# Batch 0 of a cosine-attention and FNet block: fixed load order for K and Q, squares on three engines, W1 in seven transfers

## The chip, the core and the metric

The kernel runs on one core of one Trainium2 chip. The metric is the device time of one execution in microseconds, the median of several runs. The core has TensorE (PE in the profile, with its weight loads as PEld), VectorE (DVE), ScalarE (ACT), GpSimd (POOL) and SyncE (SP). PE multiplies into PSUM. Loads and stores are DMAs; here SP issues those of K and Q and the plain stores, POOL those of V and the weights (with a cast to bf16) and the indirect stores. Each engine runs its own instructions in order and waits on semaphores.

## What is computed

For 8 batches, 12 heads, 448 tokens and heads of 64: rows of q and k are normalised, scores are divided by tau = 0.1, then softmax and the product with v. The result, 448 x 768 a batch, goes through a mixing and an FFN:

```python
q_n = q / (np.linalg.norm(q, axis=-1, keepdims=True) + 1e-06)
k_n = k / (np.linalg.norm(k, axis=-1, keepdims=True) + 1e-06)
scores = np.matmul(q_n, k_n.transpose(0, 1, 3, 2)) / tau
attn = np.exp(scores - max);  attn = attn / (sum + 1e-09)
x = np.matmul(attn, v)                       # as (8, 448, 768)
u = x + real(fft(fft(x, axis=1), axis=2))
un = (u - mean) / sqrt(var + 1e-06)
out = u + np.maximum(un @ w_ch1, 0.0) @ w_ch2    # 768 -> 3072 -> 768
```

## The kernel before

The program is not written in the order in which it runs. Every step is an operation given to a planner (`Plan.add`): the engines that may do it, an estimated cost on each, a priority, what it reads and writes. `Plan.schedule` places the operations one after another at the earliest time that its estimates give, on one of the engines allowed, and among those ready then by priority. The order it finds per engine is emitted as it is, with the semaphore waits that the reads and writes need. So the order on the chip is fixed when the kernel is built, and an engine that waits for one operation holds all behind it. `TIMES` has measured costs, `FLOW` a model of loads (latency, service time, share), `SHIFT` (lines 82 on) a number for each operation that is added to its priority. `Plan.fill` puts matmuls of the identity (later of W1) into gaps of PE; they appear as line 2168.

Batch 0 runs like this. `consts` (line 974 on) makes, with iota on POOL, arguments of cosine and sine tables: for the 448 tokens (names ending in s) and for the 768 features (ending in d). DVE reduces the arguments (lines 1014 to 1023), ACT takes the sines (1050 to 1053), with a table load for sines before and one for logarithm and exponential behind (1058). The feature table's sines come late (1050, 1052), behind batch 0's exponentials, with table loads at 1060 and 1071; `sinp` (1064) makes its negated half.

`first_norm` (line 1109 on) loads K and Q in fp32 for pairs of heads in three groups: pair 0, pairs 1 and 2, pairs 3 to 5. Each group has three loads issued by SP at line 1157: K and Q for tokens 0 to 383 and a "tail" (two DMAs, q and k of the last 64 tokens). Squares are ACT's (1164), their sums over 64 DVE's (1167). `norms` then takes the root as logarithm and exponential on ACT (1103, 1105) and the reciprocal on DVE (1106, 1107). Scaling (1186, 1190) is on DVE or POOL. PE transposes (1213, 1225 to 1227, 1238), ACT or DVE copy the result out of PSUM into QK and KTD (1204, 1248).

`attn` loads V in four pieces by POOL (1333 to 1336), behind the load with index 4 in the order of the program, which is Q of pairs 1 and 2. For each pair of heads PE makes scores (1378, 1391), ACT four exponentials into one of two buffers E (1356), three of 900 columns and one of 450. PE multiplies with V (1409, 1415), DVE divides (1433, 1435). A pair's exponentials need the product with V of the pair before the last to be done, which frees the buffer.

`fold` (1452, 1459, 1486) uses the symmetry of the transform; `fsum` does the token part on PE (1534, 1543), copied out at 1564 and 1565; `fft` the feature part (1586), in two groups, then the sum u (1650), the layer norm (1680 to 1690) and its transposition (1700, 1708). `up` is the first FFN product (1775, evacuated at 1791), `prod` the second (1919).

`weights` (line 1074) loads W1 and W2 by POOL in 12 transfers each (1084, 1085). The first three wait for the third load of V, each later one for the landing of the third before it. K and Q of batch 1 wait for the first piece of W1 (`gate` in `first_norm`).

## Time and profile before

| | us |
|---|---|
| median of 3 runs | 579.37 |
| lowest and highest | 578.66, 581.11 |
| span of the profiled execution | 579.0 |
| DVE, ACT, POOL busy in it | 438.7, 383.0, 224.5 |

The profile is one execution on the chip, shown as a page (busy time, slices, the chain that ended last, the costliest groups) and as answers to questions about its trace: a timeline of instructions, the waits, busy time by stretch, DMA issues with their time to landing. In a timeline, the bracket behind an instruction is how long its engine sat idle before it, and who ended that. A line number is that of the kernel before.

### The profile page before, as it was taken

Reading aid. Unit: us, or ns where it says so; the run is one execution under the profiler, and the core shown is the slowest. Engines: PE = TensorE matmul, PEld = TensorE weight load, DVE = VectorE, ACT = ScalarE, POOL = GpSimd, SP = SyncE. Lnnn points to the kernel's source line nnn. Section 1 sums busy time; section 2 is a strip of 40 time slices with the busy share of each in tenths; the row PEclk is TensorE's granted clock in tenths of the full one; section 3 lists DMA queues with packets and bytes.
Section 4 is the critical chain, followed back from the end, with each engine's and each line's share of the span. In section 5 each row is a group of like instructions: output and inputs, shape, how many; then the busy total and the mean of one; then the engine's idle time right before and its main releaser. Section 6 shows DMA issues by size and latency. Waiting matters only on the chain. (4 is left out here: it accounts for less than half of the span.)

```text
span 579.0 us, 16019 instructions
## 1 busy us (share of the span) xinstructions
PE 557.0 (96%) x6610; PEld 435.4 (75%) x6610; DVE 438.7 (76%) x926; ACT 383.0 (66%) x722; POOL 224.5 (39%) x338
## 2 busy tenths in 40 slices
PE   3899899999999899999999999999999999999998
PEld 3668787677687587878778678687796886959695
DVE  8789977988459967895688769976789459987353
ACT  6789967465876795479747876586558652758171
POOL 8344422446426534623362536441642103031303
PEclk9799999999999999999999999999999999999999
DMA  9999995986339652964297239942590200122011
GB/s 193 204 228 156 168 181 105 185 173 121 91 96 104 138 125 61 167 137 110 64 129 133 63 109 139 125 128 52 138 91 16 84 1 1 57 42 71 14 43 55
DMA packets 187897, 62.19 MB, mean 107 GB/s; under 512 B 166800, under 2 KB 185616, under 8 KB 187824
## 3 DMA queue, kind: packets, MB, share of 16 engines
q0 software_dynamic: 57968, 22.81, 34.6%
q1 hardware_dynamic: 129856, 38.35, 33.2%
q8 instruction: 52, 0.85, 0.6%
q14 instruction: 21, 0.17, 0.1%
HBM read 51.90 MB, written 11.01 MB: 109 GB/s over the span
## 5 line engine op out<-in xcount | busy, mean ns | idle before, releaser
L1775 PE MATMUL PS<-UNT,W1b 128*128 128x256 bf16 (+1 forms) x1728 | 186.0, 264 | 1.6 <-DVE TX L1791 0.4
L1775 PEld LDWEIGHTS PS<-UNT,W1b 128*128 128x128 bf16 x1728 | 153.1, 98 | 22.4 <-issue 2.2
L1356 ACT ACTIVATE E<-PS 128x900 bf16<-128x900 f32 (+1 forms) x192 | 148.6, 826 | 29.7 <-PE PS L1378 24.4
L1919 PE MATMUL PS<-W2b,HQ 128*128 128x384 bf16 x720 | 125.0, 326 | 0.7 <-DVE HQ L2019 0.7
L1301 POOL TENSOR_TENSOR QH<-STG,SM 128x256 bf16<-128x256 f32 x126 | 81.6, 673 | 82.6 <-DVE SM L1107 58.1
L1919 PEld LDWEIGHTS PS<-W2b,HQ 128*128 128x128 bf16 x720 | 68.8, 98 | 44.4 <-DVE HQ L2019 1.1
L1945 POOL TENSOR_TENSOR OUTB<-OUTB,U 128x192 f32<-128x192 f32 x72 | 50.8, 725 | 127.6 <-ACT OUTB L1940 111.4
L1919 PE MATMUL PS<-TX,HQ 128*128 128x384 bf16 (+2 forms) x444 | 76.7, 322 | 1.3 <-DVE OUTB L1956 1.0
L1791 ACT ACTIVATE HQ<-PS 128x512 bf16<-128x512 f32 x85 | 50.6, 595 | 40.9 <-PE PS L1775 40.2
L2019 DVE TENSOR_TENSOR HQ<-HQ 128x1536 bf16<-128x1536 bf16 (+1 forms) x73 | 56.0, 771 | 11.2 <-ACT HQ L1791 6.8
L1919 PEld LDWEIGHTS PS<-TX,HQ 128*128 128x128 bf16 x444 | 41.4, 98 | 28.0 <-DVE OUTB L1956 2.2
L1290 DVE TENSOR_REDUCE SM<-QH 128x6 f32<-128x384 f32 x84 | 45.2, 547 | 13.1 <-ACT QH L1288 12.6
L1288 ACT ACTIVATE QH<-STG 128x384 f32<-128x384 f32 x84 | 42.6, 519 | 18.9 <-DVE SM L1290 17.3
L1415 PE MATMUL PS<-VB,E 128*128 128x65 bf16 x1152 | 52.4, 194 | 0.0
...
L1415 PEld LDWEIGHTS PS<-VB,E 128*128 128x128 bf16 x1152 | 48.6, 98 | 1.3
L1791 DVE TENSOR_SCALAR HQ<-PS 128x512 bf16<-128x512 f32 x41 | 28.2, 687 | 21.7 <-PE PS L1775 21.6
L1378 PE MATMUL PS<-QK 64*128 64x225 bf16 (+2 forms) x864 | 39.4, 229 | 3.1 <-ACT QK L1204 2.0
L1409 PE MATMUL PS<-VZ,E 128*128 128x130 bf16 x192 | 41.9, 221 | 0.2
L1638 DVE SCALAR_TENSOR_TENSOR U<-ACG,X 128x768 bf16<-128x768 f32 (+4 forms) x39 | 38.9, 1006 | 0.7
L1940 ACT ACTIVATE OUTB<-PS 128x384 f32<-128x384 f32 x36 | 17.6, 490 | 31.3 <-PE PS L1919 31.3
L1378 PEld LDWEIGHTS PS<-QK 64*128 64x128 bf16 x864 | 26.0, 95 | 15.7 <-issue 8.5
...
## 6 DMA issues: line engine op xcount, KB each, us to landing
STG<-in_q_dram SPq DMA_DIRECT2D x18, 384.0 KB, 4.0
STG<-in_k_dram SPq DMA_DIRECT2D x18, 384.0 KB, 4.4
VB<-in_v_dram POOLq DMA_DIRECT2D x24, 192.0 KB, 7.1
W1b<-in_moe_w_ch_dram POOLq DMA_DIRECT2D x12, 384.0 KB, 7.8
W2b<-in_moe_w_ch_dram POOLq DMA_DIRECT2D x12, 384.0 KB, 6.7
out_dram<-OUTB SPq DMA_DIRECT2D x7, 384.0 KB, 2.9
...
```

What stands on the lines that cost most here:

```text
L1288: P.add("act", lambda a, sq=sq, src=buf[:, w * x:w * x + w]: a.activation(sq, src, ACTF.Square), t_act(w), pr, f"sq{i}_{b}", reads=bn, wri ...
L1290: P.add("dve", lambda v, o=SS[:, i, H // ns * x:H // ns * (x + 1)], sq=sq: v.tensor_reduce(o, sq.rearrange("p (h d) -> p h d", d=DH), AX.X ...
L1301: r = v.tensor_tensor(v3(qh)[:, h:h + 4], v3(buf)[:, h:h + 4], RN[:, i, h:h + 4].unsqueeze(2).to_broadcast((128, 4, DH)), AluOp.mult)
L1356: return a.activation(o, self.PS[:, bk:bk + nc_, 0:SQ2], ACTF.Exp, scale=1.0 / self.tau)
L1378: i = pe.matmul(self.PS[:, bk + h, c0:c0 + n], self.KT[r, jj, kt * 128:(kt + 1) * 128], self.QT[r, jj, cols], start=True, stop=True)
L1409: r = pe.matmul(o, st(6), self.VZ[:, j, :], start=not split, stop=(split and i == 0), skip_group_check=True)
L1415: r = pe.matmul(o[:, 65 * h:65 * h + 65], st(2 * kt + h), self.VB[:, kt, 2 * j + h, :], start=(split and i == h == kt == 0), stop=((not sp ...
L1775: r = pe.matmul(self.PS[:, bk, x * n:(x + 1) * n], self.W1b[:, j, ft * 128:(ft + 1) * 128], self.UNT[:, j, cs], start=(j == 0), stop=(j == ...
L1791: return e.activation(o, i, ACTF.Relu) if e is self.nc.scalar else e.tensor_relu(o, i)
L1919: r = pe.matmul(self.PS[:, bk, 0:n], lhs(f), rhs(f), start=(start and f == 0), stop=(stop and f == NF // 2 - 1), skip_group_check=True)
L1945: r = g.tensor_tensor(self.OUTB[:, ob, xs], self.OUTB[:, ob, xs], self.U[:, ut, xs], AluOp.add)
L2019: P.add("dve", lambda v: v.tensor_tensor(cs(o), cs(a), cs(bq), op), 0.16 + 0.3 * len(ks), -0.5, f"{nm}{ks[0]}_{b}", reads=rd, writes=[x fo ...
```

## The change

K and Q of batch 0 are loaded in the order K, Q, tail (now for pairs 0 to 2), K and Q of pairs 1 and 2, K, Q and tail of pairs 3 to 5, each load ordered behind the one before it. V waits for the landing of K of pairs 1 and 2. Squares of batch 0 may be on ACT or DVE, those of the last group on POOL too, and the last group's squares of K and Q are made pair by pair. The first arguments of the feature table may be on POOL and have a later priority; the negated sine table is read by the second group of the feature transform, and the groups change places. The first subtraction and addition of the last fold are halved, and one half needs only an earlier pair. W1 comes in two narrow and five double transfers, W2 as before. A table `HOME` fixes the engine of some 70 operations, among them the negated table and scalings of batch 0. All numbers in `SHIFT` are new, for all batches. The two iotas of the first operation are parted.

```diff
--- before.py
+++ after.py
...
 SHIFT = {
...
+HOME = {
+    "tqd": {0: "dve", 1: "dve"}, "trd": {0: "dve"}, "tas": {0: "act"}, "sinp": {0: "dve"}, "half": {0: "pool", 1: "act"}, "sqK0_0": {0: "act"},
+    "sqQ0_0": {0: "act"}, "sqT0_0": {0: "dve"}, "scK0_0": {0: "dve"}, "scQ0_0": {0: "dve"}, "scT0_0": {0: "dve"}, "ek0_0": {0: "act"},
+    "eq0_0": {0: "act"}, "et0_0": {0: "dve", 1: "act"}, "sqK1_0": {0: "dve"}, "scK1_0": {0: "dve"}, "scQ1_0": {0: "dve"}, "scT1_0": {0: "dve"},
+    "scK2_0": {0: "dve"}, "scQ2_0": {0: "dve"}, "scT2_0": {0: "dve"}, "ek1_0": {0: "dve"}, "eq2_0": {0: "act"}, "et1_0": {0: "dve", 1: "act"},
+    "sqK2_0": {1: "act", 2: "dve"}, "sqQ2_0": {0: "act", 1: "act", 2: "act"}, "sqT2_0": {0: "act"}, "scK3_0": {0: "dve"}, "scQ3_0": {0: "pool"},
+    "scT3_0": {0: "dve"}, "scK4_0": {0: "pool"}, "scQ4_0": {0: "dve"}, "scK5_0": {0: "pool"}, "scQ5_0": {0: "pool"}, "scT5_0": {0: "pool"},
+    "ek3_0": {0: "dve"}, "eq3_0": {0: "act"}, "eq4_0": {0: "dve"}, "ek5_0": {0: "act"}, "eq5_0": {0: "dve"}, "et2_0": {0: "dve"}, "gc2_0": {0: "dve"},
...
+}
...
-            g.iota(kcf, [[1, NK]], base=0, channel_multiplier=0, allow_small_or_imprecise_dtypes=True)
             for t in range(2):
                 r = g.iota(self.rowf[:, t:t + 1], [[0, 1]], base=128 * t, channel_multiplier=1, allow_small_or_imprecise_dtypes=True)
             return r
+
+        def iotak(g):
+            return g.iota(kcf, [[1, NK]], base=0, channel_multiplier=0, allow_small_or_imprecise_dtypes=True)
...
-        P.add("pool", iotas, 0.5, -19, "iota", writes=["OUT1", "OUT1b", "rowf"])
+        P.add("pool", iotas, 0.25, -19, "iota", writes=["rowf"])
+        P.add("pool", iotak, 0.4, -19, "iotak", writes=["OUT1", "OUT1b"])
...
-            m = (c.stop - c.start) // 2
+            m, es = (c.stop - c.start) // 2, ("dve", "pool") if nm == "d" else ("dve",)
             xs = [slice(c.start + t * m, c.start + t * m + m) for t in range(2)]
             for t, x in enumerate(xs):
-                P.add("dve", lambda v, x=x, t=t: v.tensor_scalar(Qt[:, x], col, self.rowf[:, k + t:k + t + 1], M, AluOp.mult, AluOp.add),
-                      t_arg(m), pr, "tq" + nm, reads=rd + ["rown"], writes=[f"tq{nm}{t}"])
+                P.add(es, lambda v, x=x, t=t: v.tensor_scalar(Qt[:, x], col, self.rowf[:, k + t:k + t + 1], M, AluOp.mult, AluOp.add),
+                      (t_arg(m), 0.2 + 0.0024 * m)[:len(es)], pr, "tq" + nm, reads=rd + ["rown"], writes=[f"tq{nm}{t}"])
             qs = [f"tq{nm}{t}" for t in range(2)]
-            P.add("dve", lambda v: v.tensor_scalar(Qt[:, c], Qt[:, c], M, -float(n), AluOp.subtract, AluOp.mult),
-                  t_arg(2 * m), pr, "tr" + nm, reads=qs, writes=qs)
+            P.add(es, lambda v: v.tensor_scalar(Qt[:, c], Qt[:, c], M, -float(n), AluOp.subtract, AluOp.mult),
+                  (t_arg(2 * m), 0.2 + 0.0048 * m)[:len(es)], pr, "tr" + nm, reads=qs, writes=qs)
...
-        arg(sd, lcf, DM, 2, -5, "d", ["OUT1d", "rowf"])
+        arg(sd, lcf, DM, 2, 16, "d", ["OUT1d", "rowf"])
...
-            done = [table(sd, self.CSd, DM, 10, "d", [trig], "CSd")]
+            done = [table(sd, self.CSd, DM, 10, "d", [trig], "CSc")]
...
-        for i in range(24):
-            c = i % 12
-
-            def fn(g, s, i=i, c=c):
-                if i < 12:
-                    return g.dma_start(self.W1b[:, :, c * 256:(c + 1) * 256], w1[:, :, c * 256:(c + 1) * 256]).then_inc(s, 16)
-                return g.dma_start(self.W2b[:, c * 2:(c + 1) * 2, :], w2[:, c * 2:(c + 1) * 2, :]).then_inc(s, 16)
-            nm = f"W{1 + i // 12}_{c}"
-            prev.append(P.add("pool", fn, 0.8, 9, nm, writes=[nm], dma=(nm, 16), after=[prev[-3]], serve=2.1))
-        self.w = prev[3:]
+        self.w = []
+        for i, (x, c0, c1) in enumerate([(0, 0, 1), (0, 1, 2)] + [(0, c, c + 2) for c in range(2, 12, 2)] + [(1, c, c + 1) for c in range(12)]):
+            def fn(g, s, x=x, c0=c0, c1=c1):
+                if x == 0:
+                    return g.dma_start(self.W1b[:, :, c0 * 256:c1 * 256], w1[:, :, c0 * 256:c1 * 256]).then_inc(s, 16)
+                return g.dma_start(self.W2b[:, c0 * 2:c1 * 2, :], w2[:, c0 * 2:c1 * 2, :]).then_inc(s, 16)
+            nm = [f"W{1 + x}_{c}" for c in range(c0, c1)]
+            prev.append(P.add("pool", fn, 0.8, 9, nm[0] if c1 - c0 == 1 else f"W1w_{c0}", writes=nm, dma=(nm[0], 16), after=[prev[-3]], serve=2.1))
+            self.w += prev[-1:] * (c1 - c0)
...
+            nt = (3, 0, 3)[g] if b == 0 else n
+            R3 = hf[:, o + 2304 + 128 * ja:o + 2304 + 128 * (ja + nt)]
             L = [("k", [(heads(K, n), self.heads(self.k, b, 2 * a, 2 * n, 0, 3, 128, 192))], 0.64 * n),
-                 ("q", [(heads(Q, n), self.heads(self.q, b, 2 * a, 2 * n, 0, 3, 128, 192))], 0.64 * n),
-                 ("t", [(heads(R[0:64], n), self.heads(self.q, b, 2 * a, 2 * n, 384, 1, 64, DH)),
-                        (heads(R[64:128], n), self.heads(self.k, b, 2 * a, 2 * n, 384, 1, 64, DH))], 0.3 * n)]
-            parts.append((g, a, n, L, [("K", K, [f"Sk{g}_{b}"]), ("Q", Q, [f"Sq{g}_{b}"]), ("T", R, [f"St{g}_{b}"])]))
+                 ("q", [(heads(Q, n), self.heads(self.q, b, 2 * a, 2 * n, 0, 3, 128, 192))], 0.64 * n)]
+            if nt:
+                L += [("t", [(heads(R3[0:64], nt), self.heads(self.q, b, 2 * a, 2 * nt, 384, 1, 64, DH)),
+                             (heads(R3[64:128], nt), self.heads(self.k, b, 2 * a, 2 * nt, 384, 1, 64, DH))], 0.3 * nt)]
+            gt = 0 if b == 0 and g == 1 else g
+            parts.append((g, a, n, nt, R3, L, [("K", K, [f"Sk{g}_{b}"]), ("Q", Q, [f"Sq{g}_{b}"]), ("T", R, [f"St{gt}_{b}"])]))
         sc, ID = [], self.ID
-        for g, a, n, L, ps in parts:
+        for g, a, n, nt, R3, L, ps in parts:
             for nm, dm, sv in L:
                 def fn(sy, sem, dm=dm):
                     for dst, src in dm:
                         sy.dma_start(dst, src).then_inc(sem, 16)
-                self.loads.append(P.add("sp", fn, 0.36 * len(dm), pg[g], f"ld_{nm}{g}_{b}", writes=[f"S{nm}{g}_{b}"],
-                                        dma=(f"lh{g}{nm}{b}", 16 * len(dm)), serve=sv, after=gate))
+                self.loads.append(P.add("sp", fn, (0.36 if b else 0.55) * len(dm), pg[g], f"ld_{nm}{g}_{b}", writes=[f"S{nm}{g}_{b}"],
+                                        dma=(f"lh{g}{nm}{b}", 16 * len(dm)), serve=sv, after=gate, order=self.loads[-1:] if b == 0 else ()))
+                if (b, g, nm) == (0, 1, "k"):
+                    self.vgate = self.loads[-1]
             red, rn = [], [[f"RN_{a + j}{i}" for j in range(n)] for i in range(3)]
             for i, (nm, buf, names) in enumerate(ps):
-                w = wd[i] * n
-                sq = sqb[i][0][:, sqb[i][1] + wd[i] * a:sqb[i][1] + wd[i] * (a + n)] if b == 0 else sqs[g][i]
-                P.add("act", lambda e, sq=sq, buf=buf: e.activation(sq, buf, ACTF.Square), t_act(w), pg[g], f"sq{nm}{g}_{b}",
-                      reads=names, writes=sqn[g][i], order=[self.exps[-1]] if b else [])
-                out = SS.rearrange("p (j c) -> p j c", c=14)[:, a:a + n, 6 * i:6 * i + (6, 6, 2)[i]]
-                red.append(P.add("dve", lambda v, sq=sq, out=out, n=n: v.tensor_reduce(out, sq.rearrange("p (j h d) -> p j h d", j=n, d=DH), AX.X, AluOp.add),
-                                 t_dve(w), pg[g], f"ss{nm}{g}_{b}", reads=sqn[g][i], writes=[f"SS_{a + j}{i}" for j in range(n)], order=sc if b else []))
+                m, y = (n, buf) if i < 2 else (nt, R3)
+                if not m:
+                    continue
+                for j0, j1 in ((0, m),) if b or g < 2 else [(j, j + 1) for j in range(m)] if i < 2 else ((0, m),):
+                    w, u0, u1 = wd[i] * (j1 - j0), wd[i] * (a + j0), wd[i] * (a + j1)
+                    sq = sqb[i][0][:, sqb[i][1] + u0:sqb[i][1] + u1] if b == 0 else sqs[g][i]
+                    y_ = y[:, wd[i] * j0:wd[i] * j1]
+                    es = ("act",) if b else (("act", "dve"), ("act", "dve"), ("act", "dve", "pool"))[g]
+                    sn = sqn[g][i] if j0 == 0 else [f"{sqn[g][i][0]}_{j0}"]
+
+                    def square(e, sq=sq, y_=y_):
+                        return e.activation(sq, y_, ACTF.Square) if e is self.nc.scalar else e.tensor_tensor(sq, y_, y_, AluOp.mult)
+                    P.add(es, square, [{"act": t_act(w), "dve": t_dve(w), "pool": 0.1 + 0.0023 * w}[e] for e in es], pg[g], f"sq{nm}{g}_{b}",
+                          reads=names, writes=sn, order=[self.exps[-1]] if b else [])
+                    out = SS.rearrange("p (j c) -> p j c", c=14)[:, a + j0:a + j1, 6 * i:6 * i + (6, 6, 2)[i]]
+                    red.append(P.add("dve", lambda v, sq=sq, out=out, n=j1 - j0: v.tensor_reduce(out, sq.rearrange("p (j h d) -> p j h d", j=n, d=DH), AX.X, AluOp.add),
+                                     t_dve(w), pg[g], f"ss{nm}{g}_{b}", reads=sn, writes=[f"SS_{a + j}{i}" for j in range(j0, j1)], order=sc if b else []))
             self.norms(b, pg[g], 14 * a, 14 * (a + n), [f"SS_{a + j}{i}" for j in range(n) for i in range(3)], rn[0] + rn[1] + rn[2])
             if b == 0:
-                self.ssk.append(red[0])
+                self.ssk += red
...
-            gate = [self.loads[4]] if b == 0 else [self.w[11]] if b == 1 else []
+            gate = [self.vgate] if b == 0 else [self.w[11]] if b == 1 else []
...
-        for i, o in ((0, AluOp.add), (2, AluOp.subtract)):
-            P.add("dve", lambda v, i=i, o=o: v.tensor_tensor(AC[:, i:i + 2], X[:, 0:2], X[:, 2:4], o),
-                  t_dve(512, 2) + (0.05 if b else 0.0), pj, f"fa{dj}_{b}", reads=xr, writes=[f"AC{i}"], after=self.snu)
+        halves = [(slice(0, 2), xr, pj, [])] if b or dj != 1 else [(slice(0, 1), [f"X{dj}"], pj - 1, self.last_f), (slice(1, 2), xr[1:], pj, [])]
+        for h, rd, pf, af in halves:
+            for i, o in ((0, AluOp.add), (2, AluOp.subtract)):
+                P.add("dve", lambda v, i=i, o=o, h=h: v.tensor_tensor(AC[:, i:i + 2, h], X[:, 0:2, h], X[:, 2:4, h], o),
+                      t_dve(256 * (h.stop - h.start), 2) + (0.05 if b else 0.0), pf, f"fa{dj}_{b}", reads=rd, writes=[f"AC{i}" + "b" * (h.start == 1)] + [f"AC{i}b"] * (h.stop == 2), after=self.snu + af)
...
-            for sg in (0, 1) if b == 0 else (0,):
+            for sg in (1, 0) if b == 0 else (0,):
                 self.fd_ops.append(P.add("pe", fn if b else lambda pe, fn=fn, sg=sg: fn(pe, sums=(sg,)), 8 * (0.085 if b == 0 else 0.064), pr + 1, f"fd{kt}_{b}",
-                                         reads=["Tt0", "Tt1", "Tt1b", "CSd"] + (["CSp"] if b == 0 and sg else []),
-                                         tiles=(tile,), acquire=None if sg else tile, margin=0.2))
+                                         reads=["Tt0", "Tt1", "Tt1b"] + (["CSp", "CSc"] if b == 0 and sg else ["CSd"] + ["CSc"] * (b == 0)),
+                                         tiles=(tile,), acquire=None if b == 0 and not sg else tile, margin=0.2))
...
+            op.engs = (HOME[op.name][k],) if k in HOME.get(op.name, ()) else op.engs
```

Left out are the numbers of `SHIFT`, the rest of `HOME`, changes of names in the fold and reads of the feature table that follow from the above, and three costs.

More of the change, by code (lines that the diff above doesn't have):

```diff
@@ L82 @@
 SHIFT = {
-    "iota": {0: -676.9695}, "cst": {0: -75.5528}, "iotad": {0: -74.6806}, "rown": {0: 48.0599}, "tqd": {0: -682.9733, 1: -32.1767},
-    "trd": {0: 56.7288}, "tpd": {0: -32.1767, 1: -367.9451}, "tad": {0: 309.9105}, "tqs": {0: -30.877, 1: -174.0331}, "trs": {0: -286.881},
[4 rows of a table removed]
-    "ldt1": {0: 105.5066}, "sind": {0: -697.7679}, "mask": {0: 897.4065}, "sinp": {0: 23.8646}, "half": {0: -44.205, 1: 289.4036},
[457 rows of a table removed]
-}
-LATE = {r"W[12]_\d+": 1.5, "tmd": 2.0, r"sq\d_\d": 1.5, r"sq[KQT]\d_1": 1.5, r"ktd\d": 2.0, r"qdup\d": 2.0, r"qk\d._[2-7]": 1.5, r"pv\d\d_[2-7]": 1.5, r"pv\d\d_1": 1.0, r"h\d+_[1-7]": 0.5}
+    "iota": {0: -4743.9411}, "iotak": {0: -3749.0012}, "cst": {0: 2295.738}, "iotad": {0: 1504.4864}, "rown": {0: 3564.9514},
@@ L1070, in tables @@
                   e.tensor_scalar(self.CSn, self.CSs[:], -1.0, None, AluOp.mult), (t_act(4 * NK), 0.5, 2.5), 10, "sinn", reads=["CSs"], writes=["CSn"])
-            self.ldt = P.add("act", lambda a: a.preload_act_table_set("natural_log_exp_and_others"), 1.3, 10, "ldt", order=done)
+            self.ldt = P.add("act", lambda a: a.preload_act_table_set("natural_log_exp_and_others"), 1.3, 28, "ldt", order=done)
         self.tables = tables
@@ L1204, in ev @@
                     return e.activation(dst, i, ACTF.Copy) if e is self.nc.scalar else e.tensor_copy(dst, i)
-                self.evac(ev, n, pg[g] + 0.1 * (jj - a), nm, b == 0 and jj > 2, writes=wr, after=(tile.users[0],), tiles=(tile,))
+                self.evac(ev, n, pg[g] + 0.1 * (jj - a), nm, False, writes=wr, after=(tile.users[0],), tiles=(tile,))
             for j in range(n):
@@ L1464, in fold @@
                 self.first_f = op
+            self.last_f = [op]
         if dj < 2 and b == 0 and not direct:
```

18 lines of the change are left out of this document (13 added, 5 removed), and 975 rows, old and new, of the table SHIFT.

## Prediction

> **What bounds the kernel now.** I read the page first: the span and the engines' shares.
>
> ```profile
> span 579.0 us, 16019 instructions
> PE 557.0 (96%) x6610; PEld 435.4 (75%) x6610; DVE 438.7 (76%) x926; ACT 383.0 (66%) x722; POOL 224.5 (39%) x338
> ```
>
> PE is busy 96% of the span, so what can be won is PE time that does no product of the result. Some of the busy time is padding: line 2168 is a matmul of the identity that only keeps PE running. So I took the busy time of each engine in three stretches, and then that of line 2168 alone (columns: stretch, us, busy us of PE, PEld, DVE, ACT and POOL; in the last two rows PE alone).
>
> ```profile
> 0.00:50.00 50.00, 36.51 (x495) 29.19 (x496) 41.05 (x97) 38.91 (x58) 26.96 (x58) 0.93 1.26 197
> 50.00:100.00 50.00, 48.01 (x662) 39.91 (x661) 40.89 (x99) 38.69 (x75) 15.44 (x22) 1.00 1.09 157
> 100.00:579.00 479.00, 472.43 (x5457) 366.25 (x5454) 356.81 (x732) 305.36 (x589) 182.12 (x260) 1.00 0.58 93
> ...
> 0.00:50.00 50.00, 12.47 (x138) 0.93 1.26 197
> 50.00:100.00 50.00, 1.50 (x18) 1.00 1.09 157
> ```
>
> Lost to PE: in the first 50 us 50 - 36.51 + 12.47 = 26.0 us, in the next 50 us 2.0 + 1.5 = 3.5, in the other 479 us 6.6. Products are the same before and after the change, so the time falls by about what the first 50 us lose less, as long as the rest stays as full as it is. That is where the edits lie; the new priorities after 100 us can win at most 6.6 us and I count them at nothing.
>
> Next the timeline of the first 53 us, by engine, to see which wait holds the attention of batch 0; here are picked rows of SP's DMA issues and of ACT (start, duration, instruction, idle time before it and who ended it).
>
> ```profile
> 0.72 0.45 SPq L1157 DMA_DIRECT2D TX<-in_q_dram  x1
> 1.23 0.49 SPq L1157 DMA_DIRECT2D TX<-in_k_dram  x1
> 1.77 1.23 SPq L1157 DMA_DIRECT2D TX<-in_q_dram  x2
> 7.69 1.28 ACT L1058 ACT_TABLE_LOAD   x1
> 8.98 0.31 ACT L1103 ACTIVATE SM<-SM,MV 128x14 f32<-128x14 f32 x1
> 16.54 0.52 ACT L1164 ACTIVATE HQ<-TX 128x384 f32<-128x384 f32 x1 [1.96 <-DMA TX<-in_k_dram]
> 16.97 0.47 ACT L1204 ACTIVATE QK<-PS 128x384 bf16<-128x384 f32 x1
> 17.91 1.73 ACT L1356 ACTIVATE E<-PS 128x900 bf16<-128x900 f32 x2 [0.47 <-PE PS L1378]
> 25.48 0.92 ACT L1356 ACTIVATE E<-PS 128x900 bf16<-128x900 f32 x1 [1.28 <-PE PS L1378]
> 33.32 7.94 ACT L1356 ACTIVATE E<-PS 128x900 bf16<-128x900 f32 x11 [0.51 <-PE PS L1378]
> ```
>
> ACT is in order. The copy of K of pair 0 (16.97) stands behind a square (16.54) that waits 1.96 us for a load of pairs 3 to 5, which pair 0 doesn't need. So the first exponential starts at 17.91; the last ends at 33.32 + 7.94 = 41.26. The first product of the FFN comes 11.1 us later:
>
> ```profile
> 52.39 5.55 PE L1775 MATMUL PS<-UNT,W1b 128*128 128x128 bf16 x96
> ```
>
> **The change part by part.** *A, the way to the first exponential.* K0, Q0 and a tail load for three pairs now lead the queue, V waits, and the arguments of the feature table leave the head of DVE.
>
> ```profile
> 9.82 0.24 DVE L1107 RECIPROCAL SM<-SM 128x14 f32<-128x14 f32 x1
> 10.62 0.54 DVE L1190 TENSOR_TENSOR QH<-TX,SM 128x384 bf16<-128x384 f32 x1
> 18.39 0.29 DVE L1186 TENSOR_TENSOR TX<-TX,SM 128x128 bf16<-128x128 f32 x1
> ```
>
> ```profile
> TX<-in_k_dram SPq DMA_DIRECT2D x1, 192.0 KB, 3.4
> TX<-in_q_dram SPq DMA_DIRECT2D x1, 192.0 KB, 3.7
> TX<-in_q_dram SPq DMA_DIRECT2D x1, 96.0 KB, 6.8
> ```
>
> With the issue times of the first three slots, K0 lands at 0.72 + 3.4 = 4.1 and Q0 at 1.23 + 3.7 = 4.9. The two DMAs of the wider tail are issued from 1.77 to 3.0; their size, 96 KB, took 6.8 in a full queue, and twice the size took 3.4 in an empty one. I take 4, nearer to the empty queue that it now has: 6.4 from the second issue at about 2.4. A square and a sum of some 0.5 each: 7.4. The table load that ended at 8.97 must also be over; it stood behind sines that waited for DVE, whose queue loses the feature table, so I let it be hidden. From the logarithm at 8.98 to the end of the reciprocal (10.06) took 1.1: 8.5. Three scalings on DVE, 0.54 + 0.29 + 0.54 = 1.4, all of pair 0 on DVE now: 9.9. Then transposing and copying Q, about 1.0 by the copy's 0.47 and as much on PE, and scores, 0.5: the first exponential at 11.4, **6.5 us** earlier. Bounds: 4.5 (the tail takes 6.8) to 7.5.
>
> V's five DMAs (POOL) move behind the landing of K1. Behind them on POOL stand iotas of the store indices, the clearing of KTD and all of W1:
>
> ```profile
> 15.60 0.88 POOL L1084 DMA_DIRECT2D W1b<-in_moe_w_ch_dram  x1 [0.55 <-POOL IDX L1036]
> 48.11 2.55 POOL L1084 DMA_DIRECT2D W1b<-in_moe_w_ch_dram  x3 [0.55 <-POOL CS L1064]
> DMA to landing us min/median/max: 5.7/7.8/11.1
> ```
>
> ```profile
> VB<-in_v_dram POOLq DMA_DIRECT2D x3, 192.0 KB, 11.5
> TX<-in_k_dram SPq DMA_DIRECT2D x1, 384.0 KB, 7.0
> GB/s 0 0 0 26 100 333 370 353 331 188 101 63 261 338 344 347 369 301 223 171 160 143 148 126 117 76 119 226 263 254 222 161 161 167 164 151 169 175 185 127
> ```
>
> The first fence is POOL's W1 issues and their time to landing; in the second, the last column of the first two lines is us to landing, and the last line is the first 20 us in slices of 0.5. K and Q alone moved at 330 to 370 GB/s at 2.5 to 4.5 us, and at 120 to 225 after 9 us, when V ran beside them. With V held back all of K and Q (2 x 12 x 448 x 64 x 4 bytes = 2.75 MB) need some 8 us at that pace: about 10. K1, fifth in the queue and issued near 3.2, lands between 6 by the pace and 10.2 by its row's 7.0. V took 11.5 from issue to landing while it shared; with less to share it should land by 17. It is first needed when the third pair's exponentials want the first buffer again, after two pairs of exponentials, some 6 us after 11.4, so it is covered by less than 1 us. If it lands later it is the next thing that is late.
>
> *B, the exponentials.* 24 are needed; by the stretch of 11 in 7.94 that is 17.3 us. The phase lasted 23.35, so 6.0 were other work and waits. In the change pair 0 starts before the squares of the later pairs are done, so more work of ACT falls inside: five squares of 0.52 (Q2 in three, T2, one of K2), two pairs of logarithm and exponential (0.5 each), four copies of 0.47: 5.5. The rest of the squares goes to DVE. Waits I put at 2.5, since no square waits for a late load in front of them. 8.0 instead of 6.0: **+2.0**. Bounds 0 to 4.
>
> Within this term lies the clock: PE did 1.89 us of work in the 4 us before it was granted half speed, and the 1.28 us wait at 25.48 falls just behind.
>
> ```profile
> 16.00:20.00 4.00, 1.89 (x25) 1.49 (x26) 2.84 (x8) 2.99 (x5) 2.38 (x5) 0.95 1.82 162
> 20.00:24.00 4.00, 3.83 (x40) 2.82 (x38) 3.65 (x7) 3.95 (x7) 0.83 (x1) 0.50 1.23 156
> ```
>
> I take the stretch of half clock to go, as the scores no longer wait for the copy at 16.97. If it only moves to the first pairs, which PE reaches after a start with little to do, that wait of about 1.3 us comes back, B is +3.3 and the time 576.2; of the forecast's chance below I give this 0.15. The Trainium skill, page "TensorE: Matmul & The Clock Gate", section "Part 1: The HAM clock gate (the "warmup" mystery)", says that a cold array runs at half rate until about 3.4 us of sustained work, and falls back after an idle window of that length; the trace agrees with the half rate, though PE was half busy, not idle, ahead of it. By that rule the 576.2 is the likelier, since PE starts idle.
>
> *C, from the last exponential to the FFN.*
>
> ```profile
> 46.00 1.15 ACT L1164 ACTIVATE OUTB<-W2b 128x1152 f32<-128x1152 f32 x1
> 47.06 0.53 ACT L1564 ACTIVATE E<-PS 65x450 bf16<-65x450 f32 x1
> 45.40 2.17 POOL L1064 TENSOR_SCALAR CS<-TX 128x770 bf16<-128x770 bf16 x1 [1.90 <-ACT TX L1052]
> 47.71 0.33 PE L1586 MATMUL PS<-TX,E 128*128 128x193 bf16 x2
> ```
>
> The feature transform starts at 47.71, right after two things: the negated sine table from POOL (ends 47.57) and the copy at 47.06, itself behind a square of batch 1. The change does the group that needs no negated table first and puts that table on DVE, so only the copy is left; freed of the square it can go some 0.5 earlier, and the half of the last fold that is done ahead takes about 0.4 more off. **-1.0**; bounds 0 and -2.
>
> *D, what is late next.* W1 landed by about 49.8 + 7.8 = 57.6 (last of three issues at 48.11), and DVE is full:
>
> ```profile
> 40.00:70.00 30.00, 28.23 (x397) 24.20 (x395) 28.63 (x75) 27.21 (x53) 14.98 (x17) 1.00 1.32 162
> ```
>
> DVE works 41.05 of the first 50 us and 28.63 of the 30 after 40. It gets four more squares of 384 columns at 0.54 each, some 2.2, and the negated table, at most POOL's 2.17, and loses some copies of about 0.5 to ACT. It has 9 us of idle time in the first 50, and 4.5 of them would go: that fits, with little slack. Seven W1 transfers instead of twelve save five POOL issues of 0.88, and POOL falls behind less often; the bytes are the same. A wide transfer isn't in the trace; I bound it by one narrow landing (7.8) and two (15.6), and take the same rate per byte. **+1.0**, bounds 0 and 6.
>
> The split of the iotas, the tail of group 1 taken from group 0's load, the gate on K1 and the halves of the fold as instructions are worth under 0.3 together, beside work of 2 us and more on their engines.
>
> The sum: -6.5 + 2.0 - 1.0 + 1.0 = -4.5, from 579.0 to 574.5. The median of the runs, 579.37, is 0.37 above the span, so **574.9**.
>
> **The rivals.** *Nothing caps it.* B and D at zero: -6.5 - 1.0 = -7.5, 571.9. For it: both terms are my estimates, and DVE and W1 just fit. Against: ACT was busy 38.91 of 50 and DVE 41.05. Chance 0.18.
>
> *The gain stays in the start-up.* Attention ends earlier, but DVE, 28.63 of 30 us busy after 40, and W1's last pieces, at their old time, let the FFN and batch 1 begin hardly earlier; the padding of line 2168 only moves. D is then 4 instead of 1: -6.5 + 2.0 - 1.0 + 4.0 = -1.5, 577.9. Against: DVE's idle time before 40 is there to be used. Chance 0.20.
>
> *W1 starts late* (the other side). V waits for K1, and W1 waits for the landing of the V load of the third token group: 8 for K1, in the middle of its bounds, 1.5 for that load's place among the V issues and 11.5 to its landing make 21 instead of 15.60. From first issue to last landing W1 took 57.6 - 15.6 = 42.0, so it ends at 63, 5.4 late; fewer POOL stalls win back 2. PE has then nothing to multiply: +3.4 on the median, 582.8. It decides from the point where W1's first issue comes later than about 18. Against: K and Q are out of V's way by then. Chance 0.12.
>
> **How the numbers follow.** My forecast has 0.50 (0.15 of it with the moved clock), with 572 to 576.4 as its own range. About 0.5% (2.9 us) is what a measurement of this kernel can tell from no change: forecast and first rival are faster by more, 0.68; the second rival is within, 0.20; the third slower, 0.12. The range goes from 569.9 (A at 7.5, C at -2, B and D at 0) to 580.5, and leaves out most of the third rival.
>
> **What would show it.** First exponential near 11.4, last near 36.8, first FFN product near 47; lost PE in the first 50 us near 21.5 instead of 26.0; no ACT square waiting over 1 us for a load behind 10 us; W1's first issue before 18 and its last landing before 56. I would be wrong if exponentials wait for V, if PE waits for W1 after 50 us, or if over 8 us are lost after 100.

## The result, and the profile after

Four runs of the kernel after have a median of 574.95 us (574.83 to 575.41), four of the kernel before on the same chip 579.31 (578.66 to 581.11): ratio 0.9926, 95% interval 0.9907 to 0.9945. Forecast were 574.9 and faster. But the sum behind that number came out right by two errors that cancel and by terms that are not where they were put. Page of the kernel after, first lines:

```profile
span 573.2 us, 16025 instructions
PE 553.7 (97%) x6616; PEld 432.9 (76%) x6616; DVE 434.0 (76%) x923; ACT 392.9 (69%) x734; POOL 224.4 (39%) x332
```

Busy time by stretch in the kernel after (columns as in the prediction), then line 2258 alone, the padding that was line 2168:

```profile
0.00:50.00 50.00, 37.81 (x545) 29.02 (x546) 43.69 (x114) 44.36 (x72) 23.14 (x53) 1.00 1.28 208
50.00:100.00 50.00, 49.06 (x651) 40.52 (x649) 40.91 (x95) 38.96 (x74) 18.40 (x24) 1.00 1.13 161
...
0.00:50.00 50.00, 12.76 (x144) 1.00 1.28 208
50.00:100.00 50.00, 1.34 (x18) 1.00 1.13 161
```

PE loses 50 - 37.81 + 12.76 = 24.95 us in the first 50 (26.0 before) and 2.3 in the next (3.5). That is 2.2 of the 5.8 by which the span fell, so lost PE time was a poor measure. Rows of ACT and PE after (as quoted of before):

```profile
7.47 1.28 ACT L1129 ACT_TABLE_LOAD   x1
9.47 0.31 ACT L1173 ACTIVATE SM<-SM,MV 128x14 f32<-128x14 f32 x1
13.30 0.94 ACT L1249 ACTIVATE HQ<-TX 128x384 f32<-128x384 f32 x2 [0.46 <-DMA TX<-in_q_dram]
15.80 2.98 ACT L1442 ACTIVATE E<-PS 128x900 bf16<-128x900 f32 x4
28.03 9.32 ACT L1442 ACTIVATE E<-PS 128x450 bf16<-128x450 f32 x13
...
48.17 5.53 PE L1864 MATMUL PS<-UNT,W1b 128*128 128x128 bf16 x96 [0.18 <-DVE UNT L1797]
```

The first exponential starts at 15.80 (17.91 before, 11.4 forecast), the last ends at 28.03 + 9.32 = 37.35 (41.26, forecast 36.8), the first FFN product comes at 48.17 (52.39, forecast 47). So the end of the phase was hit, its start missed by 4.4.

### The profile page after: what moved, and what is told of

The parts are those of the page before. It is cut to its first block, busy times and chain, and to the rows that moved or that the text cites. A ratio compares the mean times of both kernels' runs of the same rounds, so it can differ in the third digit from the quotient of the medians.

```text
span 573.2 us, 16025 instructions
## 1 busy us (share of the span) xinstructions
PE 553.7 (97%) x6616; PEld 432.9 (76%) x6616; DVE 434.0 (76%) x923; ACT 392.9 (69%) x734; POOL 224.4 (39%) x332
## 4 chain that ended last, share of the span: by engine, by line
PE 78%; DVE 8%; ACT 6%; issue 3%; POOL 2%; DMA 2%; SPq 1%; POOLq 0%; DVEq 0%; ACTq 0%
PE PS L1864 28%; PE PS L2008 26%; PE PS L1959 7%; PE PS L1501 5%; PE PS L1464 5%; PE PS L1495 2%; PE PS L1477 1%; DMA TX<-in_q_dram 1%; ACT F L1769 1%; POOL QH L1387 1%; DVE F L1547 1%; POOL OUTB L2034 1%; PE PS L1685 1%; DVE OUTB L2045 1%; DVE X L1521 1%
## 5 line engine op out<-in xcount | busy, mean ns | idle before, releaser
L1387 POOL TENSOR_TENSOR QH<-STG,SM 128x256 bf16<-128x256 f32 x126 | 84.4, 696 | 86.8 <-DVE SM L1177 65.0
L2108 DVE TENSOR_TENSOR HQ<-HQ 128x1536 bf16<-128x1536 bf16 (+1 forms) x73 | 54.1, 744 | 12.2 <-ACT HQ L1880 7.0
L2067 POOL DMA_INDIRECT out_dram<-OUTB,IDX x21 | 23.7, 1127 | 69.2 <-DVE OUTB L2045 43.4
```

Source lines behind the costliest of these rows:

```text
L1387: r = v.tensor_tensor(v3(qh)[:, h:h + 4], v3(buf)[:, h:h + 4], RN[:, i, h:h + 4].unsqueeze(2).to_broadcast((128, 4, DH)), AluOp.mult)
L2108: P.add("dve", lambda v: v.tensor_tensor(cs(o), cs(a), cs(bq), op), 0.16 + 0.3 * len(ks), -0.5, f"{nm}{ks[0]}_{b}", reads=rd, writes=[x fo ...
```

## The experiments

Theory S, the prediction's: when the first exponential starts sets when the last ends (term A). Theory W: ACT's and VectorE's queues of work set the end, whatever is first in them. A third, T, came up with the first batch of runs: much of A is a property of the one execution of before that was profiled. All edits but one change the plan between planning and emission: `at` finds the k-th operation of a name on an engine, `move` puts the first operation behind the second (with False, ahead of it), `pad` repeats a padding group, `redep` makes a padding group wait for another VectorE operation. The cuts of code below are shortened; `a`, `v` and bare names stand for operations on ACT, on VectorE and for those found by name. Each run is compared with before on its own chip; where it is set against the kernel after, the two ratios of after (0.9926, and 0.9941 below) are the measure.

| run | median, us | ratio to before (95%) | first exp. | last exp. ends | first FFN product | span |
|---|---|---|---|---|---|---|
| e1 pair 0 first | 576.72 | 0.9955 (0.9939 to 0.9971) | 14.59 | 38.72 | 49.54 | 574.9 |
| e2 table to GpSimd | 575.44 | 0.9937 (0.9920 to 0.9955) | 15.95 | 37.25 | 48.06 | 573.8 |
| e3 copies first | 578.25 | 0.9987 (0.9974 to 0.9999) | 15.96 | 37.36 | 49.58 | 575.4 |
| e4 no padding | 576.73 | 0.9951 (0.9933 to 0.9968) | 16.31 | 39.35 | 50.16 | 578.2 |
| e5 before, square late | 578.63 | 0.9994 (0.9982 to 1.0005) | 15.76 | 37.85 | 49.21 | 575.8 |
| e6 before, padded | 579.74 | 1.0020 (1.0009 to 1.0031) | 16.69 | 38.36 | 50.37 | 578.2 |
| e7 pair 0 first, padded | 576.99 | 0.9971 (0.9960 to 0.9982) | 15.01 | 38.47 | 49.33 | 575.2 |
| e8 narrow W1 | 576.64 | 0.9963 (0.9948 to 0.9977) | 16.50 | 37.93 | 48.88 | 574.8 |
| e9 before again | 578.39 (one run) | | 16.22 | 37.90 | 49.93 | 576.6 |
| e10 after again | 575.59 | 0.9941 (0.9925 to 0.9957) | 17.11 | 38.41 | 49.23 | 574.6 |
| e11 V early | 579.12 | 1.0002 (0.9991 to 1.0013) | 17.54 | 39.23 | 50.13 | 576.5 |
| e12 one copy to VectorE | 575.92 | 0.9942 (0.9928 to 0.9957) | 16.34 | 38.47 | 49.29 | 575.2 |

**Both kernels once more.** No edit.

> The kernel before, unchanged, for a second trace of it. Theory 1 (the wait of 1.96 us for the load of T2 at 16.54 and the half clock from 20 to 27 us belong to that one execution; with the same code up to there the padded kernel waited 0.33): first exponential 15.5 to 17, last exponential 37.5 to 39, first FFN product 49.5 to 51, clock 1.00, span near 576.8. Theory 2 (both are in every execution of before): 17.9, 41.3, 52.4, clock 0.994, span near 579.

> The kernel after, unchanged, on the chip of this batch, so that the edits can be set against it. Theory 1 (its start has no wait that varies by more than 0.5 us): clock 1.000 in all runs, spread under 1.5 us, first FFN product at 48 to 48.6, ratio to before 0.991 to 0.995. Theory 2 (the runs of after so far were lucky): runs at a clock under 1.000 as in before, spread of 2 us or more, ratio 0.996 or more.

Of before again (ACT, then PE):

```profile
14.85 0.52 ACT L1164 ACTIVATE HQ<-TX 128x384 f32<-128x384 f32 x1 [0.74 <-DMA TX<-in_k_dram]
16.22 1.73 ACT L1356 ACTIVATE E<-PS 128x900 bf16<-128x900 f32 x2 [0.47 <-PE PS L1378]
29.96 7.94 ACT L1356 ACTIVATE E<-PS 128x900 bf16<-128x900 f32 x11 [0.52 <-PE PS L1378]
45.25 0.33 PE L1586 MATMUL PS<-TX,E 128*128 128x193 bf16 x2 [0.75 <-POOL CS L1064]
49.93 5.54 PE L1775 MATMUL PS<-UNT,W1b 128*128 128x128 bf16 x96
```

Theory T holds. The square that waited 1.96 us at 16.54 in the prediction's profile waits 0.74 and starts at 14.85; the clock is full; the last exponential ends at 37.90, 3.4 earlier with the same program. Of after again:

```profile
12.11 0.52 ACT L1249 ACTIVATE W2b<-TX 128x384 f32<-128x384 f32 x1 [1.24 <-DMA TX<-in_k_dram]
17.11 1.73 ACT L1442 ACTIVATE E<-PS 128x900 bf16<-128x900 f32 x2
...
49.23 5.53 PE L1864 MATMUL PS<-UNT,W1b 128*128 128x128 bf16 x96 [0.18 <-DVE UNT L1797]
```

Here the load of K2 lands so that its square waits until 12.11; in the first profile of after the same square had started at 10.88. The first exponential is 1.31 later, the first FFN product 1.06, the span 1.4. So the kernel after has such a wait too (theory 1 of that run is wrong there), and what was late in the start was still late at the end. Six runs spread over 2.2 us, all at clock 1.000.

**Pair 0 first (e1, e7).** In the kernel after, its chain goes ahead on both engines, first as it is, then padded and with no load waited for ahead of it:

```diff
+redep(P, 1, v("ssQ0_0")); redep(P, 3, v("ssT0_0")); redep(P, 6, v("scQ0_0"))   # e1 and e7
+move(P, "dve", v("sqK1_0"), v("ssT0_0"))
+for n in ("ssK1_0", "sqK2_0", "ssK2_0"):          # e1; e7: ssQ1_0 behind scQ0_0, ssK1_0 before it, the other two behind it
+    move(P, "dve", v(n), v("ssQ1_0"), False)
+run = [ek0, half, eq0, et0, ln0_1, nrm0_1, ex0_0, sqQ2_0, ex0_1, sqQ2_1, ex0_2, sinn, sqQ2_2, ex0_3]   # e7; e1: ln0_1 behind ex0_0, a square of Q2 left ahead of eq0
+for x, y in zip(run, run[1:]): move(P, "act", y, x)
+redep(P, 7, v("scQ0_0")); pad(P, 7, 2)            # e7
```

> The kernel after, with ACT's and DVE's orders changed around pair 0 and no work added or taken: on DVE the square and sums of K1 and K2 go behind pair 0's sums and scalings, on ACT the copy of Q0 and the first three exponentials go ahead of two squares of Q2, the group-1 logarithm and the negated small table. Theory 1 (ACT is full from 3.8 us to the last exponential, 32.76 us busy of 37.35, so only ACT's work and idle time set the end of the exponentials): first exponential near 13.3 instead of 15.80, last exponential still at 37.0 to 37.8, time 575 +- 0.6. Theory 2 (the first exponential's start sets the end, as term A of the prediction has it): last exponential near 35, time 572.5 to 573.5.

> The kernel after, with pair 0's chain first as in the run before of that kind, but the squares of Q2 behind exponentials so that no load is waited for, the sum of Q1 ahead of those of K2, and two more groups of padding behind the first scores with none of it waiting for pair 1's reciprocal. Theory 1 (the work queued on ACT and VectorE sets the end of the exponentials, not when the first starts): first exponential 13.5 to 14.2, clock 1.00, last exponential 37.0 to 37.7, time 574.7 to 575.4. Theory 2 (the start sets the end once the clock is full): last exponential 35.5 to 36, time 573 to 573.7.

In e1 the first exponential came 1.21 earlier than in after, at 14.59, and the last 1.37 later. PE of e1, first a row of the timeline, then stretches of 2 us (us, PE busy, clock):

```profile
16.61 0.51 PE L2258 MATMUL PS<-TX 128*128 128x128 bf16 x6 [1.67 <-DVE SM L1177]
```

```profile
14.00:16.00 2.00, 0.76 (x12) 1.00 4.88 92
16.00:18.00 2.00, 1.10 (x13) 1.00 3.91 112
18.00:20.00 2.00, 2.00 (x20) 0.51 1.13 94
20.00:22.00 2.00, 2.00 (x28) 0.64 1.40 183
```

PE had little to do for 4 us and then ran at half clock. e7 keeps the clock at 1.00 in all ten runs; its first exponential is at 15.01 and its last ends at 38.47, again later than after's 37.35, and level with after again. Theory S falls for these two edits. W gave the size wrongly too: 37.0 to 37.7 was expected. With pair 0 alone in front, ACT sits between its steps (0.63 and 0.40 us for PE) instead of squaring, and 0.96 for K2's load, so the idle time is not gained but moved.

**Work off ACT (e2, e12).** In the kernel after, one operation each goes to another engine:

```diff
+move(P, "act", at(P, "act", "sinn"), at(P, "pool", "W1w_2"), to="pool")    # e2
+move(P, "act", a("ek5_0"), v("eq5_0"), to="dve")                           # e12
```

> The kernel after, with one operation moved from ACT to GpSimd: the negated copy of the small sine table (0.94 us at 11.31 on ACT) goes behind the third W1 transfer's issue on GpSimd, where that engine idles from 19.4 to 23.4. Theory 1 (ACT full): last exponential 0.9 earlier, 36.4 instead of 37.35, time 574.0 to 574.4. Theory 2 (start sets the end): the copy of K0 is what waits behind it, by at most 0.1, so first and last exponential and time stay, 575 +- 0.4. Against both: GpSimd's pass slows VectorE beside it, and the phase gets longer.

> The kernel after with one copy of 384 columns (K of pair 5, 0.49 us on ACT at 27.5, with a wait of 0.3 for it) put on VectorE behind the copy of Q5, where VectorE is idle for some 2.8 of 13.3 us; nothing else. Theory 1 (ACT's queue sets the end of the exponentials, its work and its waits; VectorE has room): last exponential 0.4 to 0.8 earlier, 36.6 to 36.9, time 0.4 to 0.8 less than after. Theory 2 (VectorE's queue of scalings is as tight): last exponential within 0.2 or later, time the same or up to 0.5 more.

Neither gains: 0.9937 and 0.9942 against 0.9926 and 0.9941. In e2 the first exponential stays (15.95), as ACT waits for VectorE (0.72) and PE (1.01) where the table was; in e12 ACT waits 0.5 for scores instead. So ACT's queue alone isn't the limit; what it no longer does it waits. Theory 2 of both runs came closer.

**The clock (e4, e6).** e4 takes the early padding from the kernel after, e6 gives before more of it:

```diff
+P.order["pe"] = [o for o in P.order["pe"] if o.name != "warm" or o.start > 19.3]    # e4
+pad(P, 8, 4)                                                                        # e6
```

> The kernel after without the padding matmuls of the identity that start before 19 us (48 or more of them between 7.56 and 19.3; the result does not use them). Theory 1 (before lost time to a stretch of half clock at 20 to 27 us that after does not have, because its padding and products leave no long gap ahead of the first exponentials): the granted clock falls to about 0.5 for some 4 us or more within 12 to 30 us, products there take half as long again or twice as long, the last exponential comes 1 to 3 us later, time 576 to 578. Theory 2 (the clock in the exponential phase costs nothing since ACT is the bound): clock falls, last exponential within 0.5, time 575 +- 0.5.

> The kernel before, with four more groups of six padding matmuls in PE's gap from 15.5 to 17.5 us, ahead of the first scores, nothing else. Theory 1 (the gap brings the half clock that the profile of before has from 20 to 27 us, and that costs time): the granted clock stays at 1.00 from 16 to 30 us and in the mean of every run, the wait of 1.28 at 25.48 goes, the runs of before at a mean clock under 0.999 (about 580.2) no longer occur, median 0.5 to 1.5 less than before. Theory 2 (ACT and VectorE hide a slow PE there): clock full, time within 0.3 of before.

The first scores of e4, then of after and of after again:

```profile
15.23 1.31 PE L1464 MATMUL PS<-QK 64*128 64x225 bf16 x12 [0.79 <-ACT QK L1290]
```

```profile
14.72 0.76 PE L1464 MATMUL PS<-QK 64*128 64x225 bf16 x12 [0.26 <-ACT QK L1290]
```

```profile
16.51 1.20 PE L1464 MATMUL PS<-QK 64*128 64x225 bf16 x12
```

Without padding the same 12 products take 1.31 instead of 0.76, and others as long again until about 25 us, although the record shows a clock of 1.00 there. But slow scores are not e4's alone: after again, which has the padding, takes 1.20, and e2, e7 and e12, with padding too, 1.31. What only e4 has is slow products beyond 20 us at a recorded clock of 1.00. Its last exponential ends 2.0 later than after's and 0.9 later than after again's, in an execution that took 580.02, the longest of seven (median 576.73). Theory 1 of e4 came closer, though the granted clock did not fall where it said. The ratio is 0.9951, 0.6 to 1.4 us above the two of after, but the intervals overlap, so what the padding is worth is not settled.

In e6 the low clock is gone (12 of 12 runs at 1.000), but the kernel is 0.2% slower than before. Two waits of e6, ACT's for the first scores and one of PE in batch 1:

```profile
16.69 1.73 ACT L1356 ACTIVATE E<-PS 128x900 bf16<-128x900 f32 x2 [1.39 <-PE PS L1378]
141.39 0.56 PE L1378 MATMUL PS<-QK 64*128 64x225 bf16 x8 [1.02 <-DMA QK<-QH]
```

The padding stands in front of the first scores, for which ACT waits 1.39 us instead of 0.47. That accounts for little: the first FFN product is 0.4 later than in before again, and 1.2 are lost behind it, 1.0 of them in the second wait, which before again does not have there. Why that transfer is late is open. Theory 1 of e6 was right on the clock and wrong on the time.

**The square that waited (e5), in the kernel before:**

```diff
+move(P, "act", a("sqT2_0"), a("sqK2_0"), False)
+move(P, "dve", v("ssT2_0"), v("ssK2_0"), False)
```

> The kernel before, with one square and its sum moved back: on ACT the square of the tail T of pairs 3 to 5 (16.54, which waited 1.96 us for its load) goes behind the first two exponentials, on VectorE its sum goes behind the scalings of pairs 1 and 2. Theory 1 (term A of the change is this one wait, and removed idle time of ACT ahead of the exponentials passes to the end): first exponential 15.7 to 16.1 as in the kernel after, last exponential 39.3 to 40.2 instead of 41.26, time 1.2 to 2.0 less than before. Theory 2 (an earlier start alone is worth nothing; VectorE's queue of sums and scalings is the next limit): first exponential early, last exponential and time within 0.5 of before.

First exponential at 15.76 as expected, time as before (0.9994): theory 2. Against before again, the last exponential ends at 37.85 instead of 37.90: the wait was only long in the profile that I had.

**Copies first (e3)**, in the kernel after:

```diff
+for k in (20, 21):
+    redep(P, k, v("gc1_0"))
+move(P, "dve", v("ssK0_1"), v("sinp"))
+move(P, "act", a("te0_0"), a("sind"))
+move(P, "act", a("te1_0"), a("te0_0"))
```

> The kernel after, with ACT's copies of the folded transform (40.24 square of batch 1, 41.30 first copy, 42.22 table load, 43.51 second copy) in the order copies, square, table load; the sum of that square on DVE goes behind the negated table. Theory 1 (the wait of the feature transform for the second copy is on the path, term C): feature transform at 42.5 or earlier instead of 44.11, first FFN product 46.5 to 47 instead of 48.17, time 573.5 to 574. Theory 2 (what is late next takes it back: VectorE's sums, W1, batch 1's norms one square later): first FFN product earlier but time 575 +- 0.5.

The feature transform starts at 43.61, 0.5 earlier than after's 44.11, and the first FFN product 1.41 later. DVE, then PE of e3:

```profile
44.21 1.35 DVE L1253 TENSOR_REDUCE SM<-OUTB 128x18 f32<-128x1152 f32 x1 [0.73 <-ACT OUTB L1249]
46.62 0.55 DVE L1739 SCALAR_TENSOR_TENSOR U<-PS,X 128x384 bf16<-128x384 f32 x1
48.41 0.51 PE L1789 MATMUL PS<-TX,F 128*128 128x128 bf16 x6 [1.93 <-DVE F L1779]
```

The square of batch 1 is late now, its sum holds VectorE's queue, and behind that sum stands the u that the layer norm needs. Theory 2, and more than it said.

**W1 in narrow transfers (e8)**, in the kernel after; the plan is unchanged, each double transfer is two DMAs (a second line makes the wait count both):

```diff
-                    return g.dma_start(self.W1b[:, :, c0 * 256:c1 * 256], w1[:, :, c0 * 256:c1 * 256]).then_inc(s, 16)
+                    return [g.dma_start(self.W1b[:, :, c * 256:c * 256 + 256], w1[:, :, c * 256:c * 256 + 256]).then_inc(s, 16) for c in range(c0, c1)][-1]
```

> The kernel after, each of the five wide W1 transfers issued as two narrow ones at the same place in GpSimd's order, waited for together: five issues of some 0.8 us more on GpSimd, the same bytes. Theory 1 (the wide transfers gave and cost nothing, term D is zero): last W1 landing within 1 us, time 575 +- 0.4. Theory 2 (the saved issues are part of the gain): GpSimd's scalings of pairs 3 to 5 come 1 to 2 us later, the exponentials of those pairs wait, time 575.5 to 577.

0.9963: slower than after by 0.2 to 0.4%, some 1 to 2 us, inside theory 2's size. But its place is not GpSimd: the first exponential is already 0.7 late, before any W1 issue, as VectorE waits 0.66 for the load of K1 (its square starts at 8.20 instead of 7.43). What wide transfers give is not settled.

**V early (e11)**, in the kernel after, on GpSimd and with the gate taken off:

```diff
+for o in loads:                      # ld_v2_0, ld_v3_0, ld_v1_0, ld_v0_0, behind vz1
+    o.deps.discard(k1); move(P, "pool", o, x); x = o
+move(P, "act", a("half"), a("ek0_0"))
+move(P, "act", a("sinn"), a("half"))
```

> The kernel after with V's five loads issued earlier: on GpSimd they go ahead of the clearing of KTD, five iotas and half a table row, and don't wait for K1; the ACT operation that waits for that half row, and the negated small table behind it, go behind the copy of K0. So V is issued from about 6.2 instead of 9.34, beside K2 and Q2. Theory 1 (V out of the way of K and Q is worth what the change gives it): K2 and Q2 land 1 to 3 us later, a square waits for them, last exponential and time 0.5 to 2 later. Theory 2 (W1 behind V is the tighter end): W1's first issue 2 to 3 us earlier than 16.94, its last landing too, and the time stays within 0.4 or falls.

The gain is gone (1.0002), but not by theory 1. Loads of K2 and Q2, of e11 and of after (last column: us to landing):

```profile
TX<-in_k_dram SPq DMA_DIRECT2D x1, 576.0 KB, 6.5
TX<-in_q_dram SPq DMA_DIRECT2D x1, 576.0 KB, 8.1
```

```profile
TX<-in_k_dram SPq DMA_DIRECT2D x1, 576.0 KB, 6.5
TX<-in_q_dram SPq DMA_DIRECT2D x1, 576.0 KB, 8.3
```

K2 and Q2 land no later with V issued at 6.44 instead of 9.34. The last tail does: its two loads take 8.7 and 8.6 us instead of 6.9 and 7.3, but no square waits for them. What is late is ACT (e11):

```profile
13.77 0.39 ACT L1138 ACTIVATE CS<-CS 1x225 bf16<-1x225 bf16 x1 [0.73 <-POOL CS L1139]
14.19 0.95 ACT L1140 ACTIVATE HQ<-CS 128x900 bf16<-128x900 bf16 x1
15.88 0.53 ACT L1290 ACTIVATE QK<-PS 128x449 bf16<-128x449 f32 x1
```

GpSimd makes its half table row behind V's issues, at 12.71 instead of 7.74; ACT's own half row and the negated table wait for it, and the copy of Q0 comes at 15.88 instead of 14.14. So it is a queue that my edit moved, and W1's first issue came only 0.2 earlier (16.72). The gate on K1 by itself isn't separated by this run; in the kernel after it did not bind, as K1, with 3.9 us to landing, was there about 7 and GpSimd came to V at 9.34.

## Why the prediction came out right, point by point

All four traces by the prediction's own stages:

| us | forecast | before to after | before again to after | before again to after again |
|---|---|---|---|---|
| A, start of the first exponential | -6.5 | -2.1 | -0.4 | +0.9 |
| B, first to last exponential | +2.0 | -1.8 | -0.1 | -0.4 |
| C, to the first FFN product | -1.0 | -0.3 | -1.2 | -1.2 |
| D and all behind it | +1.0 | -1.6 | -1.6 | -1.3 |
| span | -4.5 | -5.8 | -3.4 | -2.0 |

**The base.** The step that failed first is "the median of the runs, 579.37, is 0.37 above the span". In every run with both numbers the time is 1.75 to 1.88 above the span. By that the profiled execution of before took about 580.8, 1.4 more than the median: it had late loads and half clock. Of 68 more runs of before 16 have a mean clock under 0.999, with a median of 580.12; the other 52 have 578.57. None of the ten of after is under, which ten runs can't prove to be a rule. From the true base the sum of -4.5 gives 576.3, not 574.9; the trace pair gave -5.8. The two errors of 1.3 to 1.4 cancel.

**A** failed at three steps. "A square that waits 1.96 us for a load" was taken as the kernel's property; it was 0.74 in the next execution, and 0.33 in e6. And "the arguments of the feature table leave the head of DVE" didn't happen, they stayed ahead of the sums, with the square of K1 behind them. The third is that nothing was counted for other work between pair 0's own steps. DVE of after:

```profile
4.10 1.23 DVE L1088 TENSOR_SCALAR UNT<-UNT 128x770 f32<-128x770 f32 x1
5.44 1.14 DVE L1091 SCALAR_TENSOR_TENSOR U<-OUTB,TX,UNT 128x385 f32<-128x385 f32 x2
7.43 0.94 DVE L1249 TENSOR_TENSOR W2b<-TX 128x768 f32<-128x768 f32 x1
10.62 0.24 DVE L1177 RECIPROCAL SM<-SM 128x14 f32<-128x14 f32 x1
12.49 0.55 DVE L1276 TENSOR_TENSOR QH<-TX,SM 128x384 bf16<-128x384 f32 x1
```

ACT's part of the feature table (6.61, 0.84) also stands ahead of the table load at 7.47, and the logarithm came at 9.47 instead of 7.4: 2.1 of the 4.4 by which the start was missed. In e1, with that square of K1 moved back, it came at 8.77, right behind the table load. From the logarithm to the end of the reciprocal it took 1.4 (1.1 forecast), to the end of the scalings 2.2 (1.4), with a square and a sum of K2 between them, and from there to the first exponential 2.8 (1.5), with squares of later pairs on ACT. A later priority doesn't hold an operation back on an engine that is free for it. The landings of pair 0 were not the cause: K0 and Q0 took 2.6 instead of 3.4 and 3.7, the two loads of the first tail 3.0 and 3.4 instead of 4.

Two more slips did not decide it. The lower bound of 4.5 "(the tail takes 6.8)" adds up to 3.7, as 6.8 is 2.8 more than 4. And the row of GB/s goes from 76 to 263 after 9 us, not from 120 to 225; all of K and Q were to be there at "about 10", and the last of them landed 7.3 us after its issue at 6.96.

**B** failed as a sum of added work. ACT in the exponential phase, before again and after (columns: PE, PEld, DVE, ACT, POOL):

```profile
16.22:37.90 21.68, 19.26 (x318) 13.74 (x313) 18.83 (x42) 19.73 (x30) 8.51 (x13) 1.00 1.36 216
```

```profile
15.80:37.35 21.55, 19.40 (x322) 14.01 (x323) 18.21 (x42) 20.98 (x33) 9.29 (x11) 1.00 1.34 205
```

ACT does 1.25 more and idles 0.57 instead of 1.95: work came in, waits went out, and the length stayed. A and B are not two terms but one, where the queue of preparation ends: forecast -4.5, -3.9 between the profiles at hand, and -0.5 to +0.5 between ordinary executions. That the loads, the squares on VectorE and the gate brought batch 0's attention forward is therefore not shown.

**The half clock** was weighed rightly as a risk and wrongly as the kernel's habit: 0.50 at 20 to 24 us in the first profile, 1.00 in the second, where PE's longest gap ahead was 0.76 instead of 1.97. The feared move to the first pairs did come in after again (scores 1.20 instead of 0.76), and ACT did not wait for them. By the Trainium skill ("TensorE: Matmul & The Clock Gate", "Part 1: The HAM clock gate (the "warmup" mystery)") the array falls back after an idle window of about 3.4 us. Here it fell after PE gaps of 1.97 and 1.67 with some work around them, so the measurement decides: in these two executions a half-empty stretch was enough. Its warm-up of some 3.4 us of sustained work agrees with e4, whose products were slow until PE had run without a gap from 20.91 to some 24.7. It does not fit after again so simply: 4.3 us of padding from 7.56 on, with one gap of 0.16, left the scores at 16.51 slow, while in after the same padding was followed by products at full rate.

**C** came out near in size against before again (12.03 to 10.82), but not against the profile that it was read from (11.13), and not for its reasons. About 0.6 is the negated table, for which PE waited 0.75 in before again (it was hidden in the first profile by other lateness). The other 0.6 lies between the feature transform and the FFN (4.68 to 4.06): in before again three sums of u stood ahead of the layer norm on VectorE (46.13, 46.81, 47.29), in after two (45.00, 45.68). The last of them and the step behind it, before again, then after:

```profile
47.29 0.55 DVE L1650 SCALAR_TENSOR_TENSOR U<-PS,X 128x384 bf16<-128x384 f32 x1
47.77 0.21 DVE L1676 TENSOR_SCALAR MV<-ACG 128x1 f32<-128x1 f32 x1
```

```profile
45.68 0.56 DVE L1739 SCALAR_TENSOR_TENSOR U<-PS,X 128x384 bf16<-128x384 f32 x1
46.28 0.21 DVE L1765 TENSOR_SCALAR MV<-ACG 128x1 f32<-128x1 f32 x1
```

That the copy "is left" as what the transform waits for was right (it ends at 44.05, the transform starts at 44.11). That it gets free was wrong: it stands behind a square and a table load (40.24, 42.22). And freeing it is no gain: e3 did, won 0.5 and lost 1.9 to VectorE.

**D** had the wrong sign, and "the new priorities I count at nothing" is the larger miss. From the first FFN product to the end it takes 526.6 us in before and 526.7 in before again, 525.0 in after and 525.4 in after again. Of the ten traces with the order of after, eight lie at 525.0 to 525.9 (e11 at 526.4; e4 at 528.0, with a second low clock near 200 us), of the four with that of before, three at 526.6 to 526.7 (e6 at 527.8). Whatever the start does, this part is shorter by about 0.7 to 1.7. It lies in two places: from the first product of W2 with TX to that of TX with HQ (47.87 before, 47.43 after, both twice), and from there to the first product of line 1870, 1959 after (347.1 to 345.9 and 346.0). Both lie behind the edits of batch 0; what the change does there is another order of the plan. The last stretch to the end gives 0.3 back (89.2 to 89.5). PE's longest waits from 95 to 490 us, before again, then after again (us in total, times, longest):

```profile
PE PS L1378 <- DMA QK<-QH: 0.9, 1, 0.9
PE PS L1919 <- DVE OUTB L1956: 0.7, 1, 0.7
PE PS L1919 <- DVE HQ L2019: 0.7, 1, 0.7
```

```profile
PE PS L1495 <- issue: 1.5, 1, 1.5
PE PS L1959 <- DVE HQ L1979: 0.8, 1, 0.8
```

In the second place PE is idle 3.1 and 2.9 us in the two traces of before, 2.3 and 2.4 in those of after: waits for a DMA and for VectorE are gone, another has come, and that is half of the 1.2. Old priorities in the new kernel were not tried, so the place is shown and the cause argued. W1 capped nothing: its first issue came at 16.94, the wide transfers took 11.4 to 19.3 us to land (bounds 7.8 and 15.6), but the last piece landed at 54.1 (57.8 before, 56.3 before again), and PE does not wait for W1 after 50 us. For VectorE PE waits 0.6 in all from 49 to 110 us.

**The rivals.** That the gain stays in the start-up falls: a first FFN product 1.06 later means a span 1.4 later. That W1 starts late falls. That nothing caps it had D's size nearer, but its -6.5 was not there.

Left open: the first comparison gave 4.4 us, the second 3.2, the traces of ordinary executions 2.0 to 3.4. The low-clock runs of before explain about 16/68 x 1.55 = 0.4 of a mean; the rest is the landing of loads, in too few traces to say how much.

No edit gave a kernel faster than after.
